# Rounding a kernel's weights: the biased words in SBUF and not PSUM, a third of the early adds on VectorE, a third PSUM tile, more zero matmuls

## The chip, the cores and the metric

The kernel runs on one core of one Trainium2 chip. The time is device microseconds of one execution; the median of three runs of the kernel before was 579.76 us (577.46 to 580.57). The engines are TensorE (PE, with its weight loads as PEld), VectorE (DVE), ScalarE (ACT), GpSimd (POOL) and SyncE (SP), which issues all loads and stores.

## What is computed

Three layers of a network, all in float32, one after the other:

```
x   = attention(q, k, v)        # 2 x 8 heads, 768 positions, head size 64: each query sees 31 near keys
                                # (|i-j| < 16) and 24 block summaries (max of 32 keys, mean of 32 values)
h   = max(x @ w1, x @ w2, x @ w3)          # 1536 tokens, 512 -> 768     (layer one)
y   = h @ w_out                            # 768 -> 512                  (layer two)
out = ((y @ w_a) * (y @ w_b)) @ w_out2     # 512 -> 1536 -> 512          (layers three and four)
```

## The kernel before

A float32 product is made of three products in the format fp32r, which keeps fewer bits: both operands are split into a rounded part and a rest, and high x high, rest x high and high x rest are added in PSUM (`mm3`, line 508). Activations are split by `split` (513): ACT copies the rounded part, DVE or POOL subtracts.

The weights arrive as 64-bit words, 60 tiles of 128 x 512 words, 512 KB each. Each tile goes through three steps, numbered q = 0 to 59:

- `w_load` (415): SP issues the load into one of a few SBUF buffers (8 for the first eight, then 5 or 3 in turn). A load waits until the words that were in its buffer have been used.
- `w_round` (429) makes float32 numbers of the words. The high half is multiplied by 2^-112 ("biased"): into a PSUM tile `psw` for the first 30 tiles, in place in SBUF from then on; by ACT (line 441), for each second of three among the first 24 by DVE (line 439). ACT scales the low half in place (443). DVE shifts the biased word by 3 bits into a buffer `w` (445) and combines it with the sign bit (446). POOL adds the low half (447).
- `w_split` (455) makes the two parts of the weight: ACT copies (451), DVE or POOL subtracts (452). For the first 24 tiles, DVE does each third one and POOL the others. For layer three, sums of weight blocks are made first (467 to 470).

Tiles 0 to 17 are layer one, 18 to 23 layer two, the rest layers three and four. `weights(n)` (480) goes through the steps for n more tiles, loads some tiles ahead and rounding one ahead of splitting.

The work in order: `opening` (314) runs the attention of the first four pairs of heads and the first weights. Then the loop at line 713 goes through "turns" of layers one and two (`layers12`, 520) for four chunks of 384 tokens, with weights, and the rest of the attention in between; the attention of the second batch (`steps(1)`) begins with turn 20 and starts by loading keys (`keys`, 149), queries and values on the same SP queue, behind the weight loads issued so far. One turn of layer one is 12 matmuls into a PSUM tile of pool `ps_m`, tag "m"; after the next turn's matmuls ACT copies it out (536), or DVE takes the maximum of it and the copy (538). Layers three and four follow (`layer3`, 600, a seven-product form of 2 x 2 block products; `layer4`, 659).

PE's attention matmuls are `scores` (250), `transposes` (286), `turned` (209) and `values` (305). In the opening PE's order is fixed by `chain`; `turn_over(n)` (261) puts n matmuls of a 128 x 128 tile of zeros into it: 11 at the start, and behind each of three score steps of the groups 0 and 1 two, of 2 and 3 one.

SP's order is the program's. That of the other engines is made by a planner, which goes by the program's order, by its own estimate of times, and by how many tiles of a tag may live at once (`bufs`). The planner also lays the PSUM tiles out over the 8 banks.

Of the kernel before, what the change touches and what calls it, by code (L numbers as in the profile page):

```python
# [9 lines left out]
F32 = mybir.dt.float32  # L10
F32R = mybir.dt.float32r
I32 = mybir.dt.int32
U32 = mybir.dt.uint32
U64 = mybir.dt.uint64
AF = mybir.ActivationFunctionType
ALU = mybir.AluOpType
# [3 lines left out]
P = 128  # L20
# [5 lines left out]
NP = H // 2  # L26
# [16 lines left out]
N1, N2, NK = 3 * FF1 // P, FF1 // P, FF2 // P // 3  # L43
N12, N34 = N1 + N2, 9 * NK
# [8 lines left out]

W64, W32, WBUFS, QB, FB, SM, GB, BANKS = (5, 3), (4, 3), (24, 10), 4, (8, 2), 2, (12, 9), (2, 2, 1, 2, 2)

GATE, ROOM, SUMS, EARLY34 = (2, 3), 16, (58, 62, 66, 70), 6
TURN, ERA0, ASKS, AHEAD, PRE, TURNS = (11, 2, 1), 8, (3, 4, 5, 7, 9), (4, 1), 3, ((6, N1 - 6, 6, 4, 4, 8, N1 - 8, 4, 12), (20, 32), (32, 44))

EARLY, BIAS_DVE, SPLIT_DVE = 16, ((0, 1, 0), (0, 1, 0), (0, 0, 0)), ((0, 0, 1), (0, 0, 1), (1, 1, 1))
AT_DVE, VSUM = ((1, 0), (1, 1)), (0, 0, 0, 0, 0)


# [6 lines left out]
def attention_then_maxout_then_bilinear(ctx: ExitStack, tc: tile.TileContext, qt, kt, vt, vwin, wall, const, out):  # L77
# [3 lines left out]
    PSUM = bass.MemoryType.PSUM  # L81
    V, A, G, T = nc.vector, nc.scalar, nc.gpsimd, nc.tensor
# [3 lines left out]
    w32_p = ctx.enter_context(tc.tile_pool(name="w32", bufs=W32[0]))  # L86
# [8 lines left out]
    ps_s = ctx.enter_context(tc.tile_pool(name="ps_s", bufs=BANKS[0], space=PSUM))  # L95
    ps_t = ctx.enter_context(tc.tile_pool(name="ps_t", bufs=BANKS[1], space=PSUM))
    ps_v = ctx.enter_context(tc.tile_pool(name="ps_v", bufs=BANKS[2], space=PSUM))
    ps_c = ctx.enter_context(tc.tile_pool(name="ps_c", bufs=BANKS[4], space=PSUM))
    ps_m = ctx.enter_context(tc.tile_pool(name="ps_m", bufs=BANKS[3], space=PSUM))

    kept = one.tile([P, C_ALL + NP * NSEG * SEG], F32, name="kept")
# [32 lines left out]
    @contextmanager  # L134
    def behind_all(*names):

        with ExitStack() as held:
            for name in names:
                if name in marks:
                    held.enter_context(tc.issue_after(marks[name]))  # L140
            yield

    @contextmanager
    def chain(on=True):

        with behind_all("pe") if on else ExitStack():
            yield
# [89 lines left out]
    def scores(g, i):  # L237

        c, p = groups[g]
        t, q = CHUNKS[c][1] + i, q_t[g % QB]  # L240
        if i == 0:
            exps[g] = (sm_p.tile([P, MAXT, 2, NC], F32, tag="s", name="s"),
                       sm_p.tile([P, MAXT, 2], F32, tag="sm", name="sm"))
        s, sm = (x[:, i] for x in exps[g])
        ps = ps_s.tile([P, 2, NC], F32, tag="s", name="ps")
        nm = sm_p.tile([P, 2], F32, tag="nm", name="nm", bufs=4)
        with chain(g <= NP) if g <= NP else behind_all("first"):
            for a in range(2):
                k0 = (2 * t + a) * SEG + HALF - Z_AT[a]
                ins = T.matmul(ps[:, a], q[:, i, a], k_t[p][:, k0:k0 + NC], start=True, stop=True).ins  # L250
            if g <= NP:
                marks["pe"] = ins
        for a in range(2):
            mask = cst[:, MASK[t, a]:MASK[t, a] + NC]

            marks["scores", g, i] = V.tensor_tensor_reduce(s[:, a], ps[:, a], mask, -1.0 / D ** 0.5, 3e38, ALU.add, ALU.min, nm[:, a:a + 1]).ins  # L256
            A.activation(s[:, a], s[:, a], AF.Exp, bias=nm[:, a:a + 1], scale=-1.0, accum_out=sm[:, a:a + 1])  # L257
        if c == 0:
            turn_over(TURN[1 + p // 2])

    def turn_over(n):

        for _ in range(n):
            with chain():
                marks["pe"] = T.matmul(idle[:, 0:P], zeros, zeros, start=True, stop=True).ins
# [48 lines left out]
    def opening():  # L314
# [12 lines left out]
        for g in range(NP):  # L327
            scores(g, 0)
            if g:
                spread_(g - 1, 0)  # L330
            if g > 1:
                values(g - 2)
                load_values(g - 2 + NP)
                w_ask(ASKS[g])
            scores(g, 1)
            if g < NP - 1:
                with behind_all(("scores", g, 1), ("normal", g - 1)):
                    key_parts(0, g + 1, raw["k", g + 1])
            if g:
                transposes(g - 1)  # L340
            scores(g, 2)
            normal(g)
            if g:
                turned(g - 1)
            load(g + NP)
            if g < 2:
                w_ask(ASKS[g])
# [62 lines left out]
    w64_t, w32_t, w_t = {}, {}, {}  # L410

    def era(q):
        return 0 if q < EARLY else 1 if q < N12 else 2
# [15 lines left out]
    def w_round(q):  # L429


        r = w64_t.pop(q).bitcast(U32).rearrange("p (n t) -> p n t", t=2)
        lw, hw = r[:, :, 0], r[:, :, 1]
        to = hw.bitcast(F32)
        if q < N12 + EARLY34:

            to = ps_c.tile([P, 512], F32, tag="c", name="psw")
        if BIAS_DVE[era(q)][q % 3]:
            V.tensor_scalar(to, hw.bitcast(F32), 2.0 ** -112, None, ALU.mult)
        else:  # L440
            A.activation(to, hw.bitcast(F32), AF.Copy, scale=2.0 ** -112)
        hw = to.bitcast(U32)
        A.activation(lw.bitcast(I32), lw, AF.Copy, scale=2.0 ** -29)  # L443
        w32_t[q] = w = w32_p.tile([P, 512], F32, tag=f"w32{q < N12}", name="w32", bufs=W32[q >= N12])
        V.tensor_scalar(w.bitcast(U32), hw, 3, None, ALU.logical_shift_left)
        V.scalar_tensor_tensor(w.bitcast(U32), hw, 0x80000000, w.bitcast(U32), ALU.bitwise_and, ALU.bitwise_or)  # L446
        G.tensor_tensor(w.bitcast(I32), w.bitcast(I32), lw.bitcast(I32), ALU.add)  # L447

    def w_parts(r, eng, tag="w34", n=512):
        w = w_p.tile([P, 2, n], F32R, tag=tag, name="wt", bufs=2 if n < 512 else WBUFS[tag != "w"])  # L450
# [29 lines left out]
    def weights(most):  # L480

        nonlocal w_done, w_room
        for _ in range(most):
            if w_done == len(seq) or not fits(w_room + room[w_done]) or w_done == N12 and not gate:
                return
            w_room += room[w_done]
            w_done += 1
            ahead = min(AHEAD[0] + 2 * (w_done < ERA0 + 4), W64[w_done + AHEAD[0] > N12] - 2 * (w_done >= ERA0 + 4))
            for n, (step, more) in enumerate(((w_load, ahead), (w_round, AHEAD[1]), (w_split, 0))):
                while w_at[n] < min(w_done + more, len(seq) if gate else N12):  # L490
                    step(w_at[n])
                    w_at[n] += 1
# [300 lines left out]
```

## Time and profile before

| | |
|---|---|
| median of the runs | 579.76 us |
| profiled execution, its own time | 575.03 us |
| its span, first to last instruction | 573.3 us |
| busy: PE, DVE, ACT, POOL | 549.4, 377.1, 278.5, 202.9 us |
| granted clock of TensorE, mean | 0.988 |

The span is what the trace covers; 1.73 us of the profiled execution lie around it. Busy times are of one execution. A releaser in brackets, as "[1.29 <-ACT t L536]", says how long the engine had stood idle before an instruction and what ended last before it could start, as far as the trace shows it.

### The profile page before, as it was taken

The numbers are of one execution on the slowest core, as the hardware profiler recorded it, in microseconds if no ns is written. First come the engines' busy times: TensorE is split into PE (matmuls) and PEld (weight loads), VectorE is DVE, ScalarE is ACT, GpSimd is POOL, SyncE is SP. The second block draws the span as 40 slices with busy tenths as digits, with TensorE's granted clock in tenths as the row PEclk, the third lists the DMA queues.
The fourth block names the chain that finished last, engine by engine and source line by source line (L and its number), as shares of the span: only waits on it lengthen the run. The fifth ranks groups of instructions, "written<-read, shape, count | busy, mean of one in ns | idle before, by whom it ended". The sixth has DMA issues, their size and how long they took to land.

```text
span 573.3 us, 8967 instructions
## 1 busy us (share of the span) xinstructions
PE 549.4 (96%) x3350; PEld 518.5 (90%) x3350; DVE 377.1 (66%) x781; ACT 278.5 (49%) x667; POOL 202.9 (35%) x177
## 2 busy tenths in 40 slices
PE   8898899999999999989999799999999999999997
PEld 7788798999999999989999799899999989999985
DVE  5785988764421123767969956866768896783274
ACT  4788776854432122644655657445353544341220
POOL 4485999532110121322522513413322341330030
PEclk9988989999999999999999899999999999999999
DMA  8991368722000003211321123013122121000005
GB/s 312 355 312 49 113 212 273 234 87 92 16 1 1 0 1 111 73 38 38 119 102 43 68 74 101 31 57 109 37 74 83 65 74 38 1 0 1 0 23 198
DMA packets 16987, 51.81 MB, mean 90 GB/s; under 512 B 2096, under 2 KB 2480, under 8 KB 16944
## 3 DMA queue, kind: packets, MB, share of 16 engines
q1 hardware_dynamic: 16944, 51.25, 26.9%
q8 instruction: 26, 0.43, 0.3%
q14 instruction: 17, 0.14, 0.1%
HBM read 48.09 MB, written 3.15 MB: 89 GB/s over the span
## 4 chain that ended last, share of the span: by engine, by line
PE 66%; DVE 15%; DMA 8%; ACT 5%; POOL 3%; issue 2%; SPq 0%; POOLq 0%; DVEq 0%; ACTq 0%
PE ph L511 18%; PE qb L511 14%; PE py L511 8%; PE qg L511 5%; PE po L668 5%; PE po L667 5%; PE po L666 5%; DMA w<-wall 4%; PE qd L511 3%; DVE wt L452 3%; POOL w L447 2%; PE ps L250 2%; DMA row<-kt 2%; DVE hg L515 2%; DMA q<-qt 2%
## 5 line engine op out<-in xcount | busy, mean ns | idle before, releaser
L511 PE MATMUL ph<-x,wt 128*128 128x384 f32 x864 | 162.5, 341 | 2.3 <-ACT x L514 2.1
L511 PEld LDWEIGHTS ph<-x,wt 128*128 128x128 f32 x864 | 150.5, 190 | 3.5 <-ACT x L514 2.3
L447 POOL TENSOR_TENSOR w<-w,w 128x512 int32<-128x512 int32 x60 | 83.1, 1390 | 144.4 <-DVE w L446 72.7
L511 PE MATMUL qb<-yt,wt 128*128 128x384 f32 x576 | 113.9, 338 | 5.7 <-DVE t L637 3.2
L511 PEld LDWEIGHTS qb<-yt,wt 128*128 128x128 f32 x576 | 102.1, 188 | 11.1 <-DVE t L637 3.5
L514 ACT ACTIVATE hg<-t 128x384 fp32r<-128x384 f32 x72 | 36.9, 522 | 85.6 <-DVE t L538 40.5
L638 POOL TENSOR_TENSOR t<-t,ca 128x384 f32<-128x384 f32 x36 | 43.5, 1221 | 86.0 <-DVE t L637 83.3
L511 PE MATMUL qg<-yt,wt 128*128 128x384 f32 x288 | 59.3, 342 | 1.7 <-DVE wt L452 0.9
L678 DVE TENSOR_TENSOR acc<-po,acc 128x512 f32<-128x512 f32 x60 | 40.7, 685 | 27.2 <-PE po L668 27.1
L666 PE MATMUL po<-wt,hg 128*128 128x512 f32 x144 | 56.3, 391 | 0.5 <-ACT hg L514 0.5
L667 PE MATMUL po<-wt,hg 128*128 128x512 f32 x144 | 56.6, 393 | 0.0
L668 PE MATMUL po<-wt,hg 128*128 128x512 f32 x144 | 56.1, 395 | 0.1
L511 PEld LDWEIGHTS qg<-yt,wt 128*128 128x128 f32 x288 | 52.0, 192 | 4.0 <-DVE t L637 1.4
L511 PE MATMUL py<-hg,wt 128*128 128x384 f32 x288 | 54.2, 339 | 0.0
L515 POOL TENSOR_TENSOR hg<-t,hg 128x384 fp32r<-128x384 f32 x24 | 27.1, 1132 | 75.7 <-ACT hg L514 72.3
L538 DVE TENSOR_TENSOR t<-ph,t 128x384 f32<-128x384 f32 x48 | 26.5, 553 | 40.9 <-PE ph L511 40.2
L511 PEld LDWEIGHTS py<-hg,wt 128*128 128x128 f32 x288 | 49.9, 188 | 0.4 <-ACT y L564 0.3
L257 ACT ACTIVATE s<-s,nm 128x120 f32<-128x120 f32 x96 | 37.3, 393 | 24.2 <-DVE nm L256 24.0
L443 ACT ACTIVATE w<-w 128x512 int32<-128x512 uint32 x60 | 39.7, 668 | 9.5 <-DMA w<-wall 9.5
L515 DVE TENSOR_TENSOR hg<-t,hg 128x384 fp32r<-128x384 f32 x48 | 40.8, 861 | 3.9 <-ACT hg L514 3.8
L452 DVE TENSOR_TENSOR wt<-w,wt 128x512 fp32r<-128x512 f32 (+1 forms) x44 | 30.7, 698 | 18.0 <-ACT wt L451 17.8
L451 ACT ACTIVATE wt<-w 128x512 fp32r<-128x512 f32 (+1 forms) x60 | 34.9, 585 | 15.6 <-PE qb L511 12.5
(80 smaller groups left out, 779.5 us busy)
## 6 DMA issues: line engine op xcount, KB each, us to landing
w<-wall SPq DMA_DIRECT2D x60, 512.0 KB, 3.3
q<-qt SPq DMA_DIRECT2D x15, 384.0 KB, 6.8
row<-kt SPq DMA_DIRECT2D x8, 416.0 KB, 6.0
full<-vt SPq DMA_DIRECT2D x8, 384.0 KB, 7.0
out<-acc SPq DMA_DIRECT2D x12, 256.0 KB, 2.0
v<-vwin SPq DMA_DIRECT2D x12, 192.0 KB, 6.5
v<-vwin SPq DMA_DIRECT2D x12, 96.0 KB, 6.2
q<-qt SPq DMA_DIRECT2D x1, 256.0 KB, 4.3
```

Source lines behind the costliest of these rows:

```text
L257: A.activation(s[:, a], s[:, a], AF.Exp, bias=nm[:, a:a + 1], scale=-1.0, accum_out=sm[:, a:a + 1])
L443: A.activation(lw.bitcast(I32), lw, AF.Copy, scale=2.0 ** -29)
L447: G.tensor_tensor(w.bitcast(I32), w.bitcast(I32), lw.bitcast(I32), ALU.add)
L452: eng.tensor_tensor(w[:, 1], r, w[:, 0], ALU.subtract)
L511: T.matmul(ps, w[:, i, o:o + P], x[:, j], start=first and n == 0, stop=last and n == 2, skip_group_check=more)
L514: A.activation(dst[:, 0], src, AF.Copy)
L515: eng.tensor_tensor(dst[:, 1], src, dst[:, 0], ALU.subtract)
L638: G.tensor_tensor(t, t, cs[c, f], ALU.mult)
L666: T.matmul(ps, g[:, 0], w[:, 0], start=(f == 0), stop=False)
L667: T.matmul(ps, g[:, 0], w[:, 1], start=False, stop=False)
L668: T.matmul(ps, g[:, 1], w[:, 0], start=False, stop=(f == 1))
L678: V.tensor_tensor(acc[c, i], ps, acc[c, i], ALU.add)
```

## The change

The bias is done by ACT alone, for all tiles, and goes from the loaded words to the SBUF buffer `w`; the shift is then in place in `w`, and the combine reads the sign bit from the loaded word and not from the biased one. The PSUM pool for biased words is gone. For tiles 0, 3, 6, 9, 12 and 15 DVE makes the add of line 447 and POOL the others. Pool `ps_m` allows three tiles of a tag at once and not two. Two zero matmuls follow each score step of groups 0 to 4.

```diff
-W64, W32, WBUFS, QB, FB, SM, GB, BANKS = (5, 3), (4, 3), (24, 10), 4, (8, 2), 2, (12, 9), (2, 2, 1, 2, 2)
+W64, W32, WBUFS, QB, FB, SM, GB, BANKS = (5, 3), (4, 3), (24, 10), 4, (8, 2), 2, (12, 9), (2, 2, 1, 3)
...
-TURN, ERA0, ASKS, AHEAD, PRE, TURNS = (11, 2, 1), 8, ...
+TURN, ERA0, ASKS, AHEAD, PRE, TURNS = (11, 2, 2), 8, ...
...
-EARLY, BIAS_DVE, SPLIT_DVE = 16, ((0, 1, 0), (0, 1, 0), (0, 0, 0)), ((0, 0, 1), (0, 0, 1), (1, 1, 1))
+EARLY, ADD_DVE, SPLIT_DVE = 16, ((1, 0, 0), (0, 0, 0), (0, 0, 0)), ((0, 0, 1), (0, 0, 1), (1, 1, 1))
...
-    ps_c = ctx.enter_context(tc.tile_pool(name="ps_c", bufs=BANKS[4], space=PSUM))
     ps_m = ctx.enter_context(tc.tile_pool(name="ps_m", bufs=BANKS[3], space=PSUM))
...
-        if c == 0:
-            turn_over(TURN[1 + p // 2])
+        if g <= NP:
+            turn_over(TURN[1])
...
         lw, hw = r[:, :, 0], r[:, :, 1]
-        to = hw.bitcast(F32)
-        if q < N12 + EARLY34:
-
-            to = ps_c.tile([P, 512], F32, tag="c", name="psw")
-        if BIAS_DVE[era(q)][q % 3]:
-            V.tensor_scalar(to, hw.bitcast(F32), 2.0 ** -112, None, ALU.mult)
-        else:
-            A.activation(to, hw.bitcast(F32), AF.Copy, scale=2.0 ** -112)
-        hw = to.bitcast(U32)
+        w32_t[q] = w = w32_p.tile([P, 512], F32, tag=f"w32{q < N12}", name="w32", bufs=W32[q >= N12])
+        A.activation(w, hw.bitcast(F32), AF.Copy, scale=2.0 ** -112)
         A.activation(lw.bitcast(I32), lw, AF.Copy, scale=2.0 ** -29)
-        w32_t[q] = w = w32_p.tile([P, 512], F32, tag=f"w32{q < N12}", name="w32", bufs=W32[q >= N12])
-        V.tensor_scalar(w.bitcast(U32), hw, 3, None, ALU.logical_shift_left)
+        V.tensor_scalar(w.bitcast(U32), w.bitcast(U32), 3, None, ALU.logical_shift_left)
         V.scalar_tensor_tensor(w.bitcast(U32), hw, 0x80000000, w.bitcast(U32), ALU.bitwise_and, ALU.bitwise_or)
-        G.tensor_tensor(w.bitcast(I32), w.bitcast(I32), lw.bitcast(I32), ALU.add)
+        (V if ADD_DVE[era(q)][q % 3] else G).tensor_tensor(w.bitcast(I32), w.bitcast(I32), lw.bitcast(I32), ALU.add)
```

## Rows read from the trace of the kernel before

**Rows 1.** The page, part 1: busy time of the engines.

```profile
PE 549.4 (96%) x3350; PEld 518.5 (90%) x3350; DVE 377.1 (66%) x781; ACT 278.5 (49%) x667; POOL 202.9 (35%) x177
```

**Rows 2.** Stretches: length; busy PE, PEld, DVE, ACT, POOL; granted clock; DMA share.

```profile
10.00:45.00 35.00, 30.34 (x295) 28.15 (x296) 27.65 (x102) 25.57 (x95) 21.25 (x26) 0.95 1.02 341
...
47.31:50.72 3.41, 3.41 (x21) 3.21 (x22) 2.80 (x9) 3.41 (x12) 2.92 (x4) 0.50 0.00 0
...
56.00:88.30 32.30, 29.98 (x203) 28.64 (x204) 28.74 (x51) 24.82 (x54) 30.87 (x24) 0.95 0.44 148
...
106.00:180.00 74.00, 74.00 (x597) 70.77 (x596) 32.17 (x135) 34.74 (x124) 17.21 (x14) 1.00 0.20 61
...
276.00:573.00 297.00, 287.03 (x1483) 264.75 (x1481) 215.30 (x350) 132.68 (x262) 86.82 (x69) 0.99 0.17 60
...
320.38:323.79 3.41, 3.41 (x12) 3.41 (x12) 3.41 (x4) 1.66 (x4) 3.41 (x3) 0.50 0.00 0
```

**Rows 3.** SP's waits 40 to 130 us, chain of waits, then the timeline.

```profile
SPq L421 <- POOL w L447: 36.5, 6, 22.2
...
88.28 6.40 DMA row<-kt
...
96.17 0.71 DVE L168 COPY kept<-top 128x312 f32<-128x312 f32 x1
...
96.99 0.68 PE L250 MATMUL ps<-kept,q 128*128 128x120 f32 x4 [1.29 <-ACT t L536]
```

**Rows 4.** Lines 445 and 446: ns minimum/median/maximum, first and last start.

```profile
L445 DVE TENSOR_SCALAR w<-psw x30: 673/678/692, 28.9 to 273.0; 128x512 uint32<-128x512 uint32 x30
...
L445 DVE TENSOR_SCALAR w<-w x30: 411/418/1536, 278.9 to 491.4; 128x512 uint32<-128x512 uint32 x30
...
L446 DVE SCALAR_TENSOR_TENSOR w<-w,w x30: 675/688/1407, 279.3 to 493.4; 128x512 uint32<-128x512 uint32 x30
```

**Rows 5.** Timeline of POOL and DVE at 314 us: start, length in us.

```profile
313.77 2.63 POOL L638 TENSOR_TENSOR t<-t,ca 128x384 f32<-128x384 f32 x2
...
314.28 1.23 DVE L467 TENSOR_TENSOR s<-w 128x256 f32<-128x256 f32 x1
...
315.44 1.24 DVE L469 TENSOR_TENSOR s<-w,w 128x256 f32<-128x256 f32 x1
```

**Rows 6.** Groups by form, 56 to 88.3 us: count, busy us, mean ns, idle.

```profile
L447 POOL TENSOR_TENSOR w<-w,w 128x512 int32<-128x512 int32 x13 | 18.0, 1405 | 1.5 <-ACT s L257 1.1 <-ACT w L443 0.4
...
L452 DVE TENSOR_TENSOR wt<-w,wt 128x512 fp32r<-128x512 f32 x4 | 4.2, 1045 | 1.3 <-ACT wt L451 1.3
...
L439 DVE TENSOR_SCALAR psw<-w 128x512 f32<-128x512 f32 x4 | 2.7, 681 | 0.0
```

**Rows 7.** Timeline of PE and DVE at 83 to 87 us.

```profile
83.75 11.95 PE L511 MATMUL ph<-x,wt 128*128 128x384 f32 x68
...
86.16 0.69 DVE L445 TENSOR_SCALAR w<-psw 128x512 uint32<-128x512 uint32 x1 [0.97 <-POOL wt L452]
```

**Rows 8.** Timeline at 40 to 48 us, and two groups by form.

```profile
40.34 2.79 POOL L447 TENSOR_TENSOR w<-w,w 128x512 int32<-128x512 int32 x2 [1.20 <-ACT t L536]
...
45.04 0.66 ACT L443 ACTIVATE w<-w 128x512 int32<-128x512 uint32 x1 [4.04 <-DMA w<-wall]
...
46.24 0.61 ACT L451 ACTIVATE wt<-w 128x512 fp32r<-128x512 f32 x1
...
47.18 0.62 PE L305 MATMUL psv<-aT,v 120*64 120x64 f32 x8 [1.68 <-ACT aT L292]
...
L441 ACT ACTIVATE psw<-w 128x512 f32<-128x512 f32 x22 | 14.0, 635 | 0.6 <-DMA w<-wall 0.6
...
L265 PE MATMUL idle<-zeros 128*128 128x128 f32 x58 | 11.1, 335 | 1.1 <-DVE zeros L698 1.1
```

**Rows 9.** PE waits by line (us, times, longest); timeline at 319 us.

```profile
PE qg L511 <- DVE wt L452: 0.9, 1, 0.9
...
319.75 1.78 PE L511 MATMUL qb<-yt,wt 128*128 128x384 f32 x6 [3.19 <-DVE t L637]
```

More of the change, by code (lines that the diff above doesn't have):

```diff
@@ L52 @@
             ("S4", "B22", "g"), ("A22", "T4", "b"))
-W64, W32, WBUFS, QB, FB, SM, GB, BANKS = (5, 3), (4, 3), (24, 10), 4, (8, 2), 2, (12, 9), (2, 2, 1, 2, 2)
+W64, W32, WBUFS, QB, FB, SM, GB, BANKS = (5, 3), (4, 3), (24, 10), 4, (8, 2), 2, (12, 9), (2, 2, 1, 3)
 GATE, ROOM, SUMS, EARLY34 = (2, 3), 16, (58, 62, 66, 70), 6
-TURN, ERA0, ASKS, AHEAD, PRE, TURNS = (11, 2, 1), 8, (3, 4, 5, 7, 9), (4, 1), 3, ((6, N1 - 6, 6, 4, 4, 8, N1 - 8, 4, 12), (20, 32), (32, 44))
-EARLY, BIAS_DVE, SPLIT_DVE = 16, ((0, 1, 0), (0, 1, 0), (0, 0, 0)), ((0, 0, 1), (0, 0, 1), (1, 1, 1))
+TURN, ERA0, ASKS, AHEAD, PRE, TURNS = (11, 2, 2), 8, (3, 4, 5, 7, 9), (4, 1), 3, ((6, N1 - 6, 6, 4, 4, 8, N1 - 8, 4, 12), (20, 32), (32, 44))
+EARLY, ADD_DVE, SPLIT_DVE = 16, ((1, 0, 0), (0, 0, 0), (0, 0, 0)), ((0, 0, 1), (0, 0, 1), (1, 1, 1))
 AT_DVE, VSUM = ((1, 0), (1, 1)), (0, 0, 0, 0, 0)
```

## The prediction

> **What bounds the kernel now.** I read the page first: TensorE (PE) is busy 549.4 of 573.3 us [rows 1], so a change can win only from the 24 us in which PE stands still, from stretches of slow clock, and from the first 100 us, where PE is kept busy by small attention matmuls that wait for others. After the layer-one loop has started, PE is the bound and every microsecond that it loses is lost for good: from 106 to 180 us it has no idle time at all. The reader should therefore ask only what the change does to the moments at which PE waits.
>
> Next the busy times by stretch [rows 2]. From 56 to 88.3 us GpSimd (POOL) is busy 30.87 of 32.30 us (0.96) and VectorE (DVE) 28.74. There 13 of the 24 weights of layers one and two are rounded, and POOL, with the word adds and two of three splits, is its full engine. In 276 to 573 us POOL's share is 0.29.
>
> Then the waits of the DMA queue and the chain of waits [rows 3]. SyncE issues all loads in order. Between 40 and 130 us it waits 36.5 us for POOL's adds, since a load may only overwrite words that were added. Behind the last of these weight loads stands the first load of the second batch's keys: issued at 88.28 us, landed 6.40 us later, spread by DVE until 96.88, and PE, which had nothing else in its order, begins the scores at 96.99 after 1.29 us of waiting. So POOL's pace in 56 to 88 us is on PE's path with no slack towards late, and with only 1.29 us to win towards early.
>
> **The change, part by part.**
>
> *The shift and the combine.* For the first 30 weights the biased word went to PSUM and DVE read it there; now it stays in SBUF. The trace has both forms [rows 4]. From PSUM a shift takes 673 to 692 ns, always. From SBUF its median is 418 ns, but its maximum 1536; the combine with two SBUF inputs goes up to 1407 ns against a median of 688. What happens in the long ones is seen at 313.77 us [rows 5]: POOL runs two products, and two DVE operations that alone take about 0.42 us last 1.23 and 1.24, each until POOL's current instruction has ended. DVE operations on PSUM beside a busy POOL are not stretched. So each shift saves 0.26 us, and in return shift, combine and the new add take turns with POOL.
>
> In 56 to 88.3 us there are 13 adds [rows 6], so 13 shifts and 13 combines. Every third add of the first 16 weights goes to DVE: weights 6, 9, 12, 15, four here. Two accounts of that stretch:
> POOL's: it loses 4 x 1.405 = 5.6 us and, if it stands still whenever such a DVE operation runs, gains 13 x 0.42 + 13 x 0.69 + 4 x 0.69 = 17.3. 30.87 + 17.3 - 5.6 = 42.5 us in 32.3: late by 10.2.
> DVE's: 28.74, less 13 x 0.26 = 3.4 for shifts, less 2.7 for the four biases that go to ScalarE, plus 4 x 0.69 = 2.8 for adds; and 30 operations are held. How long? The four splits that DVE does there from SBUF average 1.045 us [rows 6], 0.36 over the 0.69 of a free one. 30 x 0.36 = 10.8. Sum 36.2 us: late by 3.9 if DVE never idles, by 7.5 if its present 3.56 us of idling stay.
> The bounds are 5.6 us early (POOL relieved, no holding) and 10.2 late. I take 6 late, near the middle of DVE's two ends, because its hold is measured in this very stretch.
>
> By the Trainium skill (SBUF — State Buffer, "Who interferes with whom") whichever of the two comes first holds the shared ports "for the whole instruction; the other fully blocks"; that covers a VectorE scalar operation in a two-port mode and one with two SBUF inputs beside a GpSimd operation that reads SBUF. By that rule POOL's account is the right one and the lateness 10.2, which is a rival below; the rows at 313 us agree with the rule, the mean hold of 0.36 us in 56 to 88 is milder.
>
> *What that does to PE.* Six microseconds move the scores of the second batch from 96.99 to 103.0 us. PE now arrives at 95.70. A third tile for layer one lets the order hold one more dense group ahead of them: 12 matmuls at 11.95 / 68 = 0.176 us [rows 7], 2.1 us. If it gives nothing (PE never waits there for an evacuation to empty a bank, and runs 68 matmuls without a gap), the 2.1 is lost; a second group would give 4.2. So + 6.0 - 2.1 = + 3.9. PE then stands 5.2 us. After the waits of 1.68 us before 47.18 and 3.19 us before 319.75 the granted clock was 0.50 for 3.41 us each time [rows 2, 8, 9]; that is the lower level, and costs half the stretch: + 1.7 (0 if the clock holds). Any delay before 95 us is absorbed in the same wait, up to 5.2 us, so I charge none separately.
>
> *Biases on ScalarE alone.* Eight instructions move from DVE (in 56 to 88 us, four of 0.68) to ACT, which takes a mean of about 0.635 for them [rows 8]: 5.1 us in all. Before 45 us this is free: ACT stands idle 4.04 us until 45.04, waiting for a weight to land, and that landing is set by DMA engines that are full from 10 to 45 us (share 1.02) [rows 2, 8]. After 45 us ACT has 7.5 us free in 56 to 88 and needs 2.5. Cost 0; if ACT's order loses that cover, 1.3 us for two. The word is now allocated by ACT's write and not by DVE's shift, so ACT, not DVE, waits when POOL has not yet split an older weight: 0.97 us once, at 86.16 [rows 7]. Behind it on ACT stand rounding copies and evacuations; that is inside the 6 us.
>
> *Zeros.* Two per score step for five groups, instead of two, two, one, one, none: 12 more, or 24 records at 11.1 / 58 = 0.19 us [rows 8], 4.6 us of PE between 13 and 41 us. They sit where PE waits for others and ahead of ACT's 4.04 us wait. Cost 0; without that cover 0.6 to 2.3 us for the last six. A slow-clock stretch that they prevent before 45 us wins nothing for the same reason.
>
> *Later.* Six more weights, rounded between 220 and 276 us, change form; 6 x 0.26 = 1.6 us of DVE. PE waits 0.9 us there for a split by DVE [rows 9]; I take two thirds, - 0.6 (bounds - 1.6, all that DVE saves, and + 2.7, if twelve operations are held 0.36 us each, 4.3, less the 1.6). From weight 30 on shift and combine already had SBUF forms, so nothing changes. In layer three more tiles do not help: PE's largest wait, the 3.19 us [rows 9], is for DVE to read a tile to which PE will go on adding.
>
> Sum: 3.9 + 1.7 - 0.6 = + 5.0 us. The profiled execution took 575.03 (span 573.3 and 1.73 around it), the median of the three runs is 579.76, 4.73 more; on the median that is 584.8.
>
> **Rivals.**
> *Faster, POOL's relief wins.* The new order loses the accident at 41 to 47 us: ACT's wait for a landing holds back the split of weight 3, whose add, the first of two in 2.79 us from 40.34, had ended near 41.7 and which ran only at 46.24 [rows 8]; PE lost 1.68 us and a slow stretch of 3.41 us behind it, 1.7. And the ring gets faster, so PE's 1.29 us at 97 goes. 579.8 - 1.7 - 1.7 - 1.3 = 575.1. It decides where the mean hold in 56 to 88 us stays under 0.11 to 0.23 us: 30 holds then equal the 3.3 us that DVE saves, without or with its idle 3.56. For it: the median of the SBUF shift, all from the stretch after 276 us, is 0.26 us under the PSUM one's. Against: POOL's share there is 0.29 and not 0.96. Chance 0.28.
> *Hidden.* The planner sets PE's order anew. If several dense groups, whose weights are long there, come ahead of the scores, late keys cost nothing: 579.8 - 0.6 = 579.2. For it: PE's 68 matmuls without a gap beside a DVE that was busy 0.89 of the time. Against: the scores come early in the program's order. Chance 0.22.
> *Full exclusion.* 10.2 us late, no group gained, one slow stretch: + 11.9, 591.7. Chance 0.12.
> The forecast itself, 581.5 to 588, has 0.38.
>
> **How the numbers follow.** Half a per cent, 2.9 us, is about what a measurement tells from no change. Slower: most of 0.38, the 0.12, a little of the hidden case: 0.49. Same: 0.20. Faster: 0.28 and some of the hidden case: 0.31. The range 573.5 to 592 reaches from the faster rival to full exclusion; a new order at 316 us could move either end by the 3.2 and 1.7 us there.
>
> **What would show it.** Shift and combine of the first weights with maxima over 1.2 us and mean holds of 0.3 or more between 56 and 90 us; POOL's adds longer than 1.405 in the mean; the keys' first load issued at 94 us instead of 88.3; a PE wait of several us near 100, and a clock of 0.5 after it. I am wrong if that load is issued before 88 us, if PE has no wait between 90 and 110, or if the wait before 47 us is gone.

## The result: 579.91 us, and the profile after

The changed kernel takes 579.91 us (median of 12 runs, 577.58 to 582.48); the kernel before, on the same chip beside it, 576.73 us (12 runs, 574.32 to 580.57). The ratio is 1.0053, 95% interval 1.0027 to 1.0079: slower by 3.2 us, about half a per cent. The forecast was + 5.0 us on a median of 579.76 us, 584.8; that median of three runs lay 3.0 us above the one of twelve. The profiled execution of after is the slowest of its twelve, 582.48 us (span 580.7), 2.6 over its median, that of before 575.03, 1.7 under its own; so the spans differ by 7.4 us where the medians differ by 3.2.

The page's busy times, and stretches of after (columns as in [rows 2]):

```profile
PE 551.3 (95%) x3374; PEld 520.8 (90%) x3374; DVE 390.7 (67%) x779; ACT 282.8 (49%) x675; POOL 203.1 (35%) x171
...
10.00:45.00 35.00, 30.00 (x296) 27.42 (x295) 29.66 (x98) 27.61 (x97) 18.85 (x24) 1.00 0.99 323
56.00:90.00 34.00, 30.86 (x230) 29.20 (x229) 32.47 (x53) 25.56 (x59) 22.95 (x16) 0.94 0.24 80
56.00:101.60 45.60, 42.46 (x297) 40.80 (x296) 43.26 (x65) 32.64 (x72) 32.10 (x22) 0.95 0.31 105
101.60:120.00 18.40, 10.16 (x48) 9.68 (x47) 17.15 (x28) 9.97 (x24) 15.14 (x11) 0.72 0.67 203
...
107.96:118.20 10.24, 5.31 (x20) 5.16 (x21) 9.10 (x12) 6.91 (x12) 8.91 (x8) 0.50 0.57 172
235.00:345.00 110.00, 110.00 (x623) 108.45 (x622) 84.48 (x130) 63.17 (x119) 39.50 (x27) 1.00 0.21 68
```

Against [rows 2] the weight work that took 32.3 us takes 45.6. The full engine has changed: DVE is busy 43.26 of 45.60 us (0.95), POOL only 32.10 (0.70, before 0.96). Then PE works 10.16 of 18.40 us, at a mean clock of 0.72. And late in the kernel, from 235 to 345 us, PE does not stand still at all. The same stretch of before:

```profile
235.00:345.00 110.00, 104.33 (x570) 100.72 (x569) 88.34 (x131) 61.70 (x117) 37.89 (x27) 0.98 0.22 72
```

So after loses in the opening and wins 5.7 us of PE time here. SP's waits and the timeline of after give the opening's loss, against [rows 3]:

```profile
SPq L420 <- POOL w L438: 41.7, 6, 27.7
...
101.62 0.42 SPq L151 DMA_DIRECT2D row<-kt  x1
...
109.98 0.94 DVE L166 TENSOR_REDUCE top<-row 128x24 f32<-128x768 f32 x1
111.66 1.13 DVE L167 COPY kept<-top 128x312 f32<-128x312 f32 x1
...
112.89 1.39 PE L249 MATMUL ps<-kept,q 128*128 128x120 f32 x5 [8.24 <-DVE kept L167]
```

The keys' first load goes 13.3 us later (101.62 against 88.28), is spread by DVE only at 112.79, and PE stands 8.24 us instead of 1.29. The clock falls to its lower level (0.50) for 10.24 us from 107.96 on. Following both traces by the n-th useful product (the zeros left out), after is 13.9 us behind at 237 us; it is 5.2 behind at 334.

The load is not all of that delay. It lands sooner after its issue than in before, 4.0 us against 6.40 (first line, of the issues at 101.62), so the keys are there at 105.62 against 94.68, 10.9 us later. In before DVE stood idle for them and took them at once (second line); in after it takes them at 109.98, over 4 us after they landed, behind weight work and 1.21 us of waiting for the next biased word of ACT (third line).

```profile
row<-kt SPq DMA_DIRECT2D x1, 416.0 KB, 4.0
...
94.70 0.95 DVE L167 TENSOR_REDUCE top<-row 128x24 f32<-128x768 f32 x1 [1.09 <-DMA row<-kt]
...
109.06 1.00 DVE L436 TENSOR_SCALAR w<-w 128x512 uint32<-128x512 uint32 x1 [1.21 <-ACT w L434]
```

Why DVE is full is in the groups by form, 56 to 90 us of after (count, busy us, mean ns, idle):

```profile
L437 DVE SCALAR_TENSOR_TENSOR w<-w,w 128x512 uint32<-128x512 uint32 x10 | 13.1, 1315 | 0.2
L443 POOL TENSOR_TENSOR wt<-w,wt 128x512 fp32r<-128x512 f32 x6 | 9.0, 1512 | 4.5 <-ACT wt L442 4.5
L438 POOL TENSOR_TENSOR w<-w,w 128x512 int32<-128x512 int32 x6 | 8.5, 1412 | 4.4 <-DVE w L437 2.5 <-issue 1.1 <-ACT t L527 0.8
L436 DVE TENSOR_SCALAR w<-w 128x512 uint32<-128x512 uint32 x11 | 8.3, 759 | 0.7 <-ACT w L434 0.7
...
L438 DVE CUSTOM_DVE_ANT_0 w<-w,w 128x1024 uint16<-128x1024 uint16 x3 | 3.5, 1164 | 0.1
```

Free, a shift takes 0.418 and a combine 0.688 us [rows 4], the add on DVE 0.68 (its shortest, below). So the holds come to 10 x 0.627 + 11 x 0.341 + 3 x 0.484 = 11.5 us in these 34. What a hold is shows in the timeline of the same stretch:

```profile
58.16 1.47 POOL L274 TENSOR_TENSOR s<-s,r 128x720 f32<-128x720 f32 x1 [3.58 <-DVE r L272]
58.42 1.76 DVE L437 SCALAR_TENSOR_TENSOR w<-w,w 128x512 uint32<-128x512 uint32 x1
...
61.17 0.68 DVE L438 CUSTOM_DVE_ANT_0 w<-w,w 128x1024 uint16<-128x1024 uint16 x1
...
62.82 1.29 POOL L443 TENSOR_TENSOR wt<-w,wt 128x512 fp32r<-128x512 f32 x1 [3.19 <-ACT wt L442]
63.11 1.55 DVE L437 SCALAR_TENSOR_TENSOR w<-w,w 128x512 uint32<-128x512 uint32 x1
...
66.00 1.58 POOL L274 TENSOR_TENSOR s<-s,r 128x720 f32<-128x720 f32 x1
66.38 1.76 DVE L437 SCALAR_TENSOR_TENSOR w<-w,w 128x512 uint32<-128x512 uint32 x1
```

POOL's instruction ends at 59.63, 64.11 and 67.58; the combine that began beside it ends at 60.18, 64.66 and 68.14, each 0.55 or 0.56 us later, however much of POOL's instruction was left when it began. So DVE's time goes up by waiting for POOL's instruction to end.

### The profile page after: what moved, and what is told of

Same layout as the page of the kernel before. It is cut to its first block, busy times and chain, and to the rows that moved or that the text cites. A ratio compares the mean times of both kernels' runs of the same rounds, so it can differ in the third digit from the quotient of the medians.

```text
span 580.7 us, 9028 instructions
## 1 busy us (share of the span) xinstructions
PE 551.3 (95%) x3374; PEld 520.8 (90%) x3374; DVE 390.7 (67%) x779; ACT 282.8 (49%) x675; POOL 203.1 (35%) x171
## 5 line engine op out<-in xcount | busy, mean ns | idle before, releaser
L502 PEld LDWEIGHTS ph<-x,wt 128*128 128x128 f32 x864 | 152.8, 193 | 4.2 <-DVE x L506 3.5
L438 POOL TENSOR_TENSOR w<-w,w 128x512 int32<-128x512 int32 x54 | 78.0, 1447 | 161.0 <-DVE w L437 91.7
L502 PE MATMUL qb<-yt,wt 128*128 128x384 f32 x576 | 115.1, 337 | 1.6 <-ACT u L612 1.0
L502 PEld LDWEIGHTS qb<-yt,wt 128*128 128x128 f32 x576 | 101.6, 188 | 6.1 <-ACT u L612 1.9
L629 POOL TENSOR_TENSOR t<-t,ca 128x384 f32<-128x384 f32 x36 | 45.0, 1267 | 64.9 <-DVE t L628 64.9
L437 DVE SCALAR_TENSOR_TENSOR w<-w,w 128x512 uint32<-128x512 uint32 x60 | 55.9, 935 | 1.0
L434 ACT ACTIVATE w<-w 128x512 f32<-128x512 f32 x60 | 39.8, 666 | 16.3 <-DVE wt L443 15.2
```

What stands on the lines that cost most here:

```text
L434: A.activation(w, hw.bitcast(F32), AF.Copy, scale=2.0 ** -112)
L438: (V if ADD_DVE[era(q)][q % 3] else G).tensor_tensor(w.bitcast(I32), w.bitcast(I32), lw.bitcast(I32), ALU.add)
L502: T.matmul(ps, w[:, i, o:o + P], x[:, j], start=first and n == 0, stop=last and n == 2, skip_group_check=more)
L629: G.tensor_tensor(t, t, cs[c, f], ALU.mult)
```

## Experiments

The theory after the result: biased words in SBUF make DVE wait for POOL, DVE becomes the full engine, the weight ring and with it the keys come late; something in the change, most likely the third tile, gives 9 us back later. Each kernel below was timed beside the kernel before on one chip; the ratio is to that, and "over before" or "under before" below means the median there. These medians of before run from 576.2 to 577.9 us, so the times of two kernels of different groups can be compared to some 1.7 us only. PE idle is 110 less its busy time from 235 to 345 us.

| kernel | us | ratio, 95% interval | keys' first load at | DVE, POOL busy of 34, 56 to 90 | PE idle 235 to 345 |
|---|---|---|---|---|---|
| before, beside after | 576.73 | 1 | 88.28 | 30.20, 32.57 | 5.67 |
| after | 579.91 | 1.0053 (1.0027 to 1.0079) | 101.62 | 32.47, 22.95 | 0.00 |
| a_bank2: after, two tiles | 588.12 | 1.0181 (1.0151 to 1.0211) | 99.70 | 32.56, 23.05 | 6.34 |
| a_psum: after, words in PSUM | 563.65 | 0.9754 (0.9727 to 0.9781) | 96.77 | 26.13, 22.91 | 0.85 |
| a_zeros: after, old zeros | 578.65 | 1.0019 (0.9995 to 1.0043) | 97.82 | 31.59, 23.25 | 0.00 |
| a_early8: after, keys earlier | 576.56 | 0.9998 (0.9967 to 1.0029) | 86.54 | 32.36, 23.98 | 0.02 |
| b_words: before, words in SBUF | 592.62 | 1.0246 (1.0213 to 1.0279) | 95.46 | 32.71, 29.70 | 6.24 |
| b_sign: before, sign from SBUF | 583.57 | 1.0124 (1.0083 to 1.0165) | 94.22 | 32.62, 30.19 | 6.02 |
| b_words_w5_gb11: b_words, fifth w32 | 592.56 | 1.0280 (1.0242 to 1.0317) | 95.70 | 33.79, 29.58 | 5.44 |
| b_add: before, DVE's adds | 578.70 | 1.0028 (0.9998 to 1.0059) | 92.22 | 33.69, 26.87 | 5.68 |
| b_bank3: before, third tile | 564.15 | 0.9794 (0.9762 to 0.9826) | 90.15 | 30.64, 33.48 | 1.05 |
| b_bank4: before, four tiles | 562.66 | 0.9754 (0.9712 to 0.9796) | 90.31 | 32.31, 32.66 | 1.98 |

### The parts undone or done alone

**a_bank2**

```
-BANKS = ... (2, 2, 1, 3)
+BANKS = ... (2, 2, 1, 2)
```

> After with two PSUM tiles for the dense stage instead of three. Theory (the biased words in SBUF make VectorE and GpSimd take turns, the weight ring turns later, and the second batch's keys, behind it in SP's order, with it): the keys' first load is issued at 99 to 104 us as in after (101.62), and TensorE waits 5 to 10 us for the spread near 110. What this run tells apart is how some 9 of the 14 us of lateness come back between 236 and 334 us: if the third tile gives them back, the time is 584 to 589 us (after 579.9); if the planner gives back any lateness of the opening, 578 to 582. Rival (the third tile reorders the dense work and that is what makes the keys late): load at 87 to 92 and about 577 us.

588.12 us, and the opening as late as in after (13 us by the n-th product from 113 us on). But this kernel keeps its lateness to the end (12.8 at 237, 11.8 at 334, 13.4 at 548), where after wins 8.7 back. The wait of [rows 9] is there again, with a smaller one behind it (timeline of PE):

```profile
331.23 1.31 PE L502 MATMUL qb<-yt,wt 128*128 128x384 f32 x6 [2.45 <-DVE t L628]
334.64 0.62 PE L502 MATMUL qg<-yt,wt 128*128 128x384 f32 x2 [1.05 <-DVE t L628]
```

It is the third tile that gives the time back: 8.2 us in after by the medians, 7.4 by the two ratios.

**a_psum** (the lines on the words of the first 30 tiles; the shift reads `hw` again, and from tile 30 on the word is biased in place, as in before)

```
-w = w32_p.tile(...)                         # biased word, in SBUF
-A.activation(w, hw, Copy, scale=2.0 ** -112)
+to = ps_c.tile([P, 512], F32, tag="c")      # one PSUM bank, bufs=1
+A.activation(to, hw, Copy, scale=2.0 ** -112)
+hw = to
```

> After with the biased words back in PSUM (one bank, ScalarE alone writes them), everything else of the change kept: VectorE's adds, the third tile, the zeros. Theory: the shift takes 0.67 to 0.75 us and the sign's instruction 0.65 to 0.72 on the mean between 56 and 90 us (after 0.75 and 1.25), the keys' first load goes at 86 to 92 us, TensorE waits under 3 us for its spread, and the time is 571 to 576 us, 4 to 9 under after. Rival (VectorE's adds and the third tile do it, the words are nearly free): load still at 97 to 103 us, time 578 to 582.

563.65 us, 16.3 under after and outside the expected range on the good side. The two instructions in their PSUM form, groups of 56 to 90 us, then the stretch:

```profile
L441 DVE TENSOR_SCALAR w<-psw 128x512 uint32<-128x512 uint32 x11 | 7.5, 686 | 3.9 <-ACT psw L437 3.7
L442 DVE SCALAR_TENSOR_TENSOR w<-psw,w 128x512 uint32<-128x512 uint32 x10 | 6.9, 687 | 0.2
...
56.00:90.00 34.00, 34.00 (x231) 32.97 (x231) 26.13 (x44) 24.04 (x54) 22.91 (x18) 0.97 0.35 125
```

No combine is held (longest of the 30 with a PSUM source: 0.694 us), DVE has 6.3 us less to do in these 34, and PE stands still not once. The keys' load was expected at 86 to 92 us and went at 96.77, yet nothing waits for it:

```profile
94.83 8.48 PE L507 MATMUL ph<-x,wt 128*128 128x384 f32 x48
104.08 1.51 PE L507 MATMUL ph<-x,wt 128*128 128x384 f32 x7 [0.76 <-DVE t L534]
105.42 1.05 PE L250 MATMUL ps<-kept,q 128*128 128x120 f32 x8
```

Ahead of these scores PE has 307 dense products in its order (264 in after, 240 in before) and its weights in time for them. Late keys alone cost nothing here; where the dense work in front of them runs out first, PE waits (8.24 us in after, 11.39 in b_words).

**a_zeros**

```
-turn_over(TURN[1])  if g <= NP,  TURN = (11, 2, 2)
+turn_over(TURN[1 + p // 2])  if c == 0,  TURN = (11, 2, 1)
```

> After with the zeros of before (two or one products after a score group of the first pass, none after the fifth head pair). Theory: the zeros are beside the matter, keys' load at 100 to 104 us, time 579 to 581 (within 1.5 us of after). Rival (the zeros keep the clock up in the opening): one or two more stretches of 3.41 us at clock 0.5 before 75 us and 581 to 584; other rival (the zeros stand in the way of useful products): 577 to 579.

578.65 us: 1.3 under after, with intervals that overlap; the value lies in the second rival's range, but can't be told from no effect. There are two clock stretches at 0.50 before 45 us (10.24 us in all) that after doesn't have; after has one of 6.83 us from 49.94 on instead. So the zeros move the slow clock in the opening and are worth nothing measurable, as the prediction had it.

**b_words**: the same four lines of the words as in after, ScalarE alone, and nothing else of the change.

> Before with one part alone: the biased words of the early weights stay in SBUF and ScalarE alone writes them; GpSimd adds all words, two dense tiles, old zeros. Theory: the sign's instruction rises from 0.68 to over 1.0 us on the mean between 56 and 90, the keys' first load goes at 96 us or later (before 88.28), TensorE waits over 4 us near 105, and the time is 579 to 587 us if the late opening isn't given back by another part, over before in any case. Rival (the words are free and the late keys come from VectorE's adds or the third tile): load at 86 to 91, 575 to 578 us.

592.62 us, 14.7 over before: beyond the expected 579 to 587. Groups of 56 to 90 us, and PE's wait:

```profile
L437 DVE SCALAR_TENSOR_TENSOR w<-w,w 128x512 uint32<-128x512 uint32 x11 | 14.4, 1320 | 0.2
L436 DVE TENSOR_SCALAR w<-w 128x512 uint32<-128x512 uint32 x10 | 10.1, 1018 | 0.2 <-ACT w L434 0.2
...
109.36 2.04 PE L249 MATMUL ps<-kept,q 128*128 128x120 f32 x8 [11.39 <-ACT w L434]
```

Holds: 11 x 0.632 + 10 x 0.600 = 13.0 us. The words alone cost more than the whole change.

**b_bank3**

```
-BANKS = (2, 2, 1, 2, 2)
+BANKS = (2, 2, 1, 3, 2)
```

> Before with one part alone: a third PSUM tile for the dense stage (the words' two PSUM tiles stay). Theory: the third tile is worth about what its removal from after cost (588.1 less 579.9 is 8.2 us): 567 to 572. Rival (it is worth that only when the opening is late, as in after, by more dense work ahead of the late keys): 575 to 579.

564.15 us, 12.5 under before, more than expected. By the n-th product it is 3.8 us ahead at 237 us and 11.1 ahead at 334.

```profile
56.00:90.00 34.00, 32.08 (x221) 30.58 (x220) 30.64 (x54) 25.53 (x54) 33.48 (x26) 1.00 0.46 156
235.00:345.00 110.00, 108.95 (x600) 105.19 (x599) 86.26 (x132) 67.16 (x131) 35.21 (x27) 1.00 0.24 81
```

In 235 to 345 us PE idles 1.05 us instead of 5.67 and the clock stays at 1.00. The order of work there is another: layer two's last product starts at 283.4 us (before 298.0), layer four's first at 315.4 (before 299.7).

**b_add**

```
-G.tensor_tensor(w, w, lw, ALU.add)
+(V if ADD_DVE[era(q)][q % 3] else G).tensor_tensor(w, w, lw, ALU.add)   # (1, 0, 0) in the first era
```

> Before with one part alone: VectorE instead of GpSimd adds every third of the first 16 weights' words. Before with the SBUF words alone took 592.6, and the SBUF words with VectorE's adds and the zeros 588.1 (after with two tiles), so these two parts are worth some 4.5 us there. Theory (the adds take GpSimd, busy 32.57 of the 34 us from 56 to 90 in before, off its limit): 570 to 575, GpSimd under 28 us of those 34. Rival (VectorE is as full, 30.20 of 34, and takes up what GpSimd gives): 576 to 580.

578.70 us, no gain, the rival's value: POOL falls from 32.57 to 26.87 of 34 us, and DVE rises from 30.20 to 33.69. POOL's relief by itself is worth nothing, because DVE was nearly as full. Beside the SBUF words it may be worth something (a_bank2 has the adds and the zeros over b_words, and is 4.5 us faster), which wasn't parted from the zeros.

**b_bank3_act**: b_bank3 with ScalarE alone writing the biased words, in PSUM.

> Before with the third dense tile (564.15 us) and with ScalarE alone writing the biased words, which stay in PSUM. VectorE loses every third biasing instruction in the opening (0.68 us each, about eight of them), where it is 30.6 of 34 us busy. Theory (VectorE's weight work sets the opening): 558 to 563. Rival (the opening's 4 us are gone already with the third tile, the rest is hidden): 563 to 566.

564.96 us, ratio 0.9795 (0.9758 to 0.9833), as b_bank3: the theory's 558 to 563 was missed. Moving the biases costs and gives nothing.

### Holding or the w32 tile?

That the words cost so much could also come from ScalarE taking the w32 tile earlier than the shift did. Two kernels part the two.

**b_sign**: words in PSUM as before; only the sign is read elsewhere.

```
-V.scalar_tensor_tensor(w, hw,     0x80000000, w, bitwise_and, bitwise_or)   # hw: biased, PSUM
+V.scalar_tensor_tensor(w, raw_hw, 0x80000000, w, bitwise_and, bitwise_or)   # raw_hw: as loaded, SBUF
```

> Before with one operand moved: the biased words stay in PSUM, written as in before, and the shift reads them there, but the instruction that puts in the sign takes its sign from the loaded words in SBUF (the sign is the same), so its two sources are in SBUF while the number of tiles, the order of the work and the engines stay. It parts the two ways in which the words in SBUF could slow the weight ring. Theory A (an instruction of VectorE with both sources in SBUF and one of GpSimd make each other wait): the sign's mean between 56 and 90 us rises from 0.68 to over 1.0 us, the keys' first load goes 2 to 10 us later than 88.28, and the time is 579 to 588. Theory B (the ring is slow because ScalarE now takes the w32 tile, and no longer the shift after it): this kernel is as before, 575.5 to 578, the sign under 0.75.

583.57 us, 7.2 over before, from one operand. Groups of 56 to 90 us:

```profile
L447 DVE SCALAR_TENSOR_TENSOR w<-w,w 128x512 uint32<-128x512 uint32 x12 | 14.0, 1172 | 0.0
L446 DVE TENSOR_SCALAR w<-psw 128x512 uint32<-128x512 uint32 x11 | 7.3, 681 | 0.3 <-ACT psw L442 0.3
```

With its second SBUF source the combine goes from 0.680 to 1.172 us (12 x 0.49 = 5.9 us in the stretch), the shift from PSUM beside it stays at 0.681, and the keys go 5.9 us later (94.22 against 88.28). That is theory A.

**b_words_w5_gb11**

```
-W32 = (4, 3); GB = (12, 9)
+W32 = (5, 3); GB = (11, 9)
```

> Before with the biased words in SBUF (592.6 us) and a fifth w32 tile for them, paid for with one of the twelve tiles of the dense stage's activations. Theory A (turn-taking of VectorE and GpSimd): the sign's mean stays over 1.0 us, the keys' first load stays at 94 us or later, and the time is 588 to 596. Theory B (the w32 tile taken earlier): the keys' load goes at 87 to 91 and the time falls to 576 to 584.

592.56 us, the combine at 1.318 us and the keys' load at 95.70: a fifth tile, at the price of one for activations, brings nothing. What that price is wasn't measured, so a small gain could hide behind it; but b_sign has the holds and 7.2 us of loss without any change in the w32 tiles, and theory B isn't needed.

### Are the keys behind the ring the whole of the opening's loss?

**a_early8** (and **b_early8**, the same in before): the second batch's first loads are asked for at group 8 of the dense loop instead of 20.

```
         next(dense[int(c)])
+        if i == 8:
+            with tc.issue_after(mark[0]):
+                next(todo)
+            done = 1
```

> After with one edit: the second batch's first keys, queries and values are asked for at the ninth group of the dense stage instead of the twenty-first, which puts their loads in front of the last four weight loads in SP's order. Theory (the keys stand behind the late weight ring in SP's order, and that alone is the wait of 8.24 us): the keys' load goes at 87 to 91 us (after 101.62), the wait for the spread near 105 falls under 3 us, the stretch at clock 0.5 after it goes too, and the time falls by 5 to 12 us, to 568 to 575. Rival (VectorE, busy 43.26 of the 45.6 us from 56 to 101.6, is the bound: the keys' maxima and spreads, moved into that stretch, push its weight work back by as much): the wait moves to another place and the time stays at 577 to 583.

576.56 us: 3.4 under after, between the theory's 568 to 575 and the rival's 577 to 583. The load goes at 86.54, and PE waits elsewhere instead:

```profile
100.12 0.28 PE L194 MATMUL psvs<-kept,mean 128*24 128x128 f32 x1 [3.10 <-DVE mean L183]
...
117.58 0.70 PE L250 MATMUL ps<-kept,q 128*128 128x120 f32 x4 [1.68 <-DVE kept L168]
```

At 237 us this kernel is still 8.5 us late, where after is 13.9. So some 5 us of the opening's loss is the place of the keys in SP's order. The larger part stays with the keys early; that it is DVE's own work is argued from its 32.36 busy us of 34, which are as in after, and not shown by a run.

> Before with the same edit: the second batch's first loads four weight loads earlier. TensorE waited there 1.29 us for the spread alone, so the theory gives at most 1 to 3 us: 574 to 578. Rival (the early keys take VectorE's time from the weights that TensorE waits for): 578 to 582.

b_early8: 578.95 us, ratio 1.0065 (1.0038 to 1.0091), the rival's time, though its keys went at 78.78 us: in before the keys' place costs nothing. The rival's reason is not shown: PE's waits of over 1.2 us between 60 and 120 us are for DVE's `x` (1.62), `mean` (1.99) and `t` (1.38) there, none for a weight.

### Where the third tile wins

**b_bank4** has four tiles (BANKS 4 in the place of 3).

> Before with four dense tiles instead of three. If the third tile works by giving the planner of the instruction order more freedom, a fourth gives some more: 559 to 563. If what it took away is all that was to be had (TensorE's waits between 236 and 334 us are at 1 us already), or PSUM's eight banks are the limit: 563 to 567.

562.66 us, the fastest that was run; its interval overlaps those of a_psum (0.9754) and b_bank3 (0.9794), so the three can't be ranked.

In the next kernels the third tile has a tag of its own, which every third group must take, and is given only to a part of the dense work: to the first batch's layers one and two (01), the second batch's (23), layer four's (po), to the last two, or to all.

```
+if part not in THIRD: return ps_m.tile([P, 512], F32, tag="m", name=name)
+turn_of[part] = n = (turn_of.get(part, -1) + 1) % 3
+return ps_m.tile([P, 512], F32, tag="mmn"[n], name=name, bufs=(2, 2, 1)[n])
```

> Before with a third PSUM tile, of a tag of its own, for every third group of the first batch's dense chunks only (0 and 1, the work between 33 and some 160 us). The third tile in all dense work gave 12 us: by the n-th product 4 of them by 237 us and 7 more between 236 and 334. If the two gains are separate, this kernel has the first: 571 to 574 us, and still TensorE's waits between 236 and 334 us (5.6 us in before, 3.19 of them for VectorE's read of a layer-three tile). If the whole gain comes from a new order of the opening, all 12: 563 to 567. If the tile must be had by all: 576 to 579.

b_third_01: 572.48 us, ratio 0.9941 (0.9916 to 0.9966). It is 4.2 us ahead at 237 us and still 4.0 at 548, and the wait is there:

```profile
315.54 1.90 PE L517 MATMUL qb<-yt,wt 128*128 128x384 f32 x5 [3.07 <-DVE t L643]
```

The opening's gain is a thing by itself, some 4 us.

> Before with the third tile for the second batch's dense chunks only (2 and 3, from some 160 to 298 us). If the gain between 236 and 334 us comes from the dense groups that are mixed with the first layer-three products: 568 to 571 us, without the 3.19 us wait near 317. The forecast's own claim (the waits there are for tiles of layer three, which stay as they are): 575 to 578 with that wait.

> Before with the third tile for the products of layer four only (from some 300 us on). If the gain between 236 and 334 us comes from layer four's groups, which can then stand between two products of layer three: 568 to 571 us, without the 3.19 us wait. If not: 575 to 578, with it.

> Before with the third tile for the second batch's dense chunks and for layer four, not for the first batch. Alone, neither was worth anything (576.7 and 577.0). If the 7 us between 236 and 334 come from both having it together: 568 to 571, and no wait over 1 us between 236 and 334. If they need the first batch's tile too: 575 to 578.

576.70, 577.03 and 575.25 us, ratios 1.0000 (0.9978 to 1.0022), 1.0007 (0.9981 to 1.0033) and 0.9966 (0.9934 to 0.9998); PE's idle time in 235 to 345 us stays at 5.39, 6.44 and 5.78 us. None shows the 7 us.

> The control: a third tile of a tag of its own for all dense work, which should be as three tiles of one tag (564.15 us): 562 to 567. If it is above 570, the form with a second tag was itself the reason for the small gains of the three runs before.

The control took 570.32 us, ratio 0.9859 (0.9807 to 0.9911), idle 3.31 us: a third tile that every third group must take is worth about three fifths of one that any group may take (7.4 us against 12.5). So the negative results of the three runs before it don't prove that their part of the work has no share. What stays open is which dense work brings the late gain; that it comes from the free third tile is shown by the table: all kernels with it idle 0.0 to 2.0 us in 235 to 345, all with two tiles 5.4 to 6.3. How it does so is open too: b_third_23po has a new order as well (layer two's last product starts at 288.5 us, layer four's first at 304.0) and keeps its idle time.

## Why the forecast was right in direction and wrong in size

**Right: the chain.** Words in SBUF, holds, a slow ring, keys behind it, PE's wait near 100 us, slow clock after it: each was named, each is in the trace of after, and b_words, b_sign and a_psum show the words as its cause. Of the signs that the prediction named, POOL's longer adds came weakly (1.412 us in 56 to 90 against 1.405), and one spoke against it: the wait before 47 us is gone. Another stands in its place, and a slow stretch of 6.83 us goes with it:

```profile
50.53 1.21 PE L249 MATMUL ps<-kept,q 128*128 128x120 f32 x4 [3.00 <-DVE nm L255]
```

So the forecast's faster rival was right that this wait would go, and won nothing by it.

**Too small: "I take 6 late".** The keys' load was 13.3 us late. The step that failed first is the mean hold of 0.36 us, which I took from four splits of DVE in the trace of before [rows 6]. It measured 0.48 over the 24 operations between 56 and 90 us of after (11.5 / 24) and 0.62 over the 21 of b_words (13.0 / 21). I had read the shape of a hold correctly at 314 us [rows 5], until POOL's current instruction has ended, but priced it by a mean from a few operations in another order. The groups of after over the whole stretch, 56 to 101.6 us:

```profile
L437 DVE SCALAR_TENSOR_TENSOR w<-w,w 128x512 uint32<-128x512 uint32 x14 | 17.4, 1251 | 0.2
L436 DVE TENSOR_SCALAR w<-w 128x512 uint32<-128x512 uint32 x14 | 10.6, 754 | 1.5 <-ACT w L434 1.5
L438 DVE CUSTOM_DVE_ANT_0 w<-w,w 128x1024 uint16<-128x1024 uint16 x4 | 5.0, 1248 | 0.1
```

Over the free times these are 14 x 0.563 + 14 x 0.336 + 4 x 0.568 = 14.9 us of holds, 4.1 more than the 10.8 forecast. DVE's busy time, 43.26, is 7.0 over the 36.2 of the forecast; the other 2.9 are work that the forecast's count didn't hold (one more shift and combine, more of the first batch's attention). DVE's own account was the right one in kind, with DVE as the full engine; POOL wasn't (32.10 of 45.60 us), so the 5.6 us early bound, POOL relieved, was no bound on this path at all, as b_add shows.

**At nothing: DVE's delay of the spread.** The forecast moved PE's scores by the same 6 us as the load. They started 15.9 us later (112.89 against 96.99): the landing 10.9 later, and 5.0 more until DVE had spread the keys. Against it stood two dense groups and not one (264 products against 240, 4.2 us where 2.1 was forecast), and the slow clock cost some 2.7 us and not 1.7. 15.9 - 4.2 + 2.7 = 14.4, near the 13.9 that after is behind at 237 us; the forecast had 5.6.

The full-exclusion rival, from the Trainium skill (SBUF — State Buffer, "Who interferes with whom"), gave 10.2 us late, nearer to the 13.3 than my 6, though by POOL's account, in which POOL is busy for 42.5 us; it was busy for 32.10, so the number is near by luck. The same section of the Trainium skill says that a VectorE instruction with at most one SBUF input, outside the two-port modes, does not contend; the trace agrees: with one source in PSUM the 30 combines of a_psum last 0.673 to 0.694 us, with both in SBUF the 60 of after 0.675 to 1.765.

**Wrong: "in layer three more tiles do not help", and - 0.6 for all that is later.** This is the step that made the forecast too slow. The late gain was - 8.7 us (13.9 late at 237, 5.2 at 334); a_bank2 shows that two tiles win back only 1.0 there. I argued from the wait itself, which is for DVE's read of a tile to which PE will add. But with a third tile the planner writes another order, and in it PE doesn't stand at that moment; whether the order does it, or the free tile at run time, was not parted. The prediction names "a new order at 316 us" as able to move an end by 3.2 and 1.7; it did so, in one direction, and I gave it no weight in the sum. In the opening the tile was costed at - 2.1; alone it gave about - 4.

**Hidden.** Its 579.2 us is the rival's value nearest to the 579.91, but its mechanism isn't what after shows, where PE waited 8.24 us for the keys. It is what a_psum shows, with 307 products ahead of the scores.

**Right by bounds: zeros and biases.** Costed at 0; a_zeros is 1.3 us from after with overlapping intervals, b_bank3_act 0.8 from b_bank3.

The errors have opposite signs. Alone, the words cost 14.7 us, DVE's adds 2.0 (an interval that touches zero), and the tile gives 12.5: together + 4.2, near the 3.2 measured. The forecast had about 7 and 2 for words and tile, + 5.0. It was near because both were halved or worse, not because either was known; that was luck. Nor do the parts add up exactly: tile and DVE's adds alone come to - 10.5, but a_psum, which has both and the zeros, with the words in one PSUM tile and not two, is 14.3 under before.

## What to carry to other kernels

Before moving an operand of VectorE from PSUM to SBUF, look at what GpSimd does at that time: where it is busy most of the stretch, each such instruction with two SBUF sources may wait for a whole GpSimd instruction, and a bias in PSUM that looks like a detour is what keeps the engines apart. When a change bundles parts, price each alone with its own row; here one part of a slower kernel was worth 12.5 us by itself, and undoing one other part (a_psum) beats both kernels by over 2%. And where an order is planned, a spare output tile is worth trying even if no wait names it.

## What the runs showed of the hardware that was not expected

- A held DVE instruction ends a fixed time after POOL's. Of the weight instructions of DVE from SBUF that lasted over 1.1 us in before, after, b_words and a_psum, 156 in all, every one began while a POOL instruction ran and ended 0.28 to 0.29 or 0.54 to 0.56 us after a POOL instruction did: the first value for the shift and for the 256-wide sums and splits, the second for the two-source instructions 512 wide.
- POOL is held as well. Of its adds that began between 56 and 102 us in before, after, b_words and b_sign, 31 began while a weight instruction of DVE from SBUF ran, and 30 of these lasted 1.36 to 1.85 us (one 1.30); the other 25 lasted 1.29 to 1.34. In b_words 13 of 14 adds are such, in before 3 of 18.
- The integer add of 128x512 words on DVE is in the trace as one instruction on 128x1024 uint16, 0.68 us when free, against 1.29 to 1.34 us for the same add on POOL when it isn't held (mean with the held ones 1.41 [rows 6]).
- With the wait of 8.24 us the lower clock lasted 10.24 us, where the waits of 1.68 and 3.19 us in before had 3.41 each [rows 2, 8, 9]; with the wait of 3.00 us in after it lasted 6.83. PE was busy 5.31 us of the 10.24, so they cost about half of that, an estimate of 2.7 us, where the forecast charged 1.7.
